# Attention with top-32 and two MLP layers on one core: VectorE's written order from unit 2 on, and three small differences moved between engines

## The chip, the cores and the metric

The kernel runs on one NeuronCore of a Trainium2 chip. The metric is device time in microseconds; the median of three runs of the kernel before is 1382.83 us (1382.4 to 1383.42).

The engines are named as in the profile: PE is TensorE (matrix multiply, writes PSUM), DVE is VectorE, ACT is ScalarE, POOL is GpSimd, SP is SyncE, which issues most DMAs.

## The reference

```python
def _attn_ref(q, k, v):                      # q, k, v: [4, 8, 576, 64] float32
    scores = scale * np.matmul(q, k.transpose(0, 1, 3, 2))
    kth = np.partition(scores, -32, axis=-1)[..., -32:-31]
    scores = np.where(scores >= kth, scores, -1000000000.0)
    attn = np.exp(scores - np.max(scores, axis=-1, keepdims=True))
    attn = attn / (np.sum(attn, axis=-1, keepdims=True) + 1e-09)
    return np.matmul(attn, v)

def _moe_ref(x, w_in, w_out, a, b):          # x: [2304, 512]; w_in: [512, 2048]; w_out: [2048, 512]
    h = x @ w_in
    P = a[0] + a[1] * h + a[2] * h**2 + a[3] * h**3
    Q = 1.0 + np.abs(b[0]) * np.abs(h) + np.abs(b[1]) * h**2
    return (P / (Q + 1e-6)) @ w_out

def _moe2_ref(x, w_in, w_out):               # the same sizes
    h = x @ w_in
    return (h * np.cos(h)) @ w_out
```

The attention's output, laid out as 2304 tokens of 512, goes through `_moe_ref` and then `_moe2_ref`.

## The kernel before

**Units and pieces.** The attention is cut into 72 units, each a tile of 128 query rows of a pair of heads. Each unit is written as five pieces, and the program is a run of pieces: piece p belongs to unit p // 5. The MLP layers work on 9 blocks of 256 tokens; block k's first layer starts at piece 46 + 40 k (unit 9 for block 0), its second layer 50 pieces later, so from about unit 19 on a block's worth of both layers runs beside every 8 units of attention.

**A unit.** PE makes the scores (`qk`, tile `sx`), ACT copies them to `sS`. DVE searches the 32nd largest of each row (`topk`): two TENSOR_TENSOR (maximum and minimum of the row's two halves) into `e`, then MAX8 and MATCH_REPLACE8 in turn, while ACT makes the exponentials into `e`; two SCALAR_TENSOR_TENSOR then mask `e` and sum it, PE transposes it (`pp`) and multiplies it with v (`av`). The scores take q and k in two parts each, a high part rounded for TensorE's faster kind of float32 and the rest as a low part. q is split for two units at once (`split_q`): ACT writes `qh`, and the difference `ql` is made by DVE from unit 20 on and by GpSimd before it. `qh` has one buffer, so ACT may overwrite it only when PE has done the scores of the unit that still reads it.

**Conversion.** The four weight matrices arrive as 64-bit floats, and 64 conversions (`conv`, 128x512 each) turn them into such pairs of parts. Kinds 0 and 1 are the first layer's input and output weights, kinds 2 and 3 those of the second. One conversion is: DMA of `raw`; two ACT operations (`cb<-raw`, `raw<-raw`); a shift by DVE (`TENSOR_SCALAR cb<-cb`); an integer add by GpSimd (`cb<-cb,raw`); the high part by ACT; the difference from the high part; two DMAs to DRAM, from which the layers read it later. The difference is made by PE for kinds 0 and 2 (two matmuls into `diff`, one with the identity and one with its negative, then an ACT copy `cb<-diff`), by GpSimd for kind 1 and by DVE for kind 3 (`cb<-cb,ch`). Kinds 0 and 1 have six `cb` buffers; kinds 2 and 3 have three, so the first ACT operation of a conversion waits until the difference of the third one before it has landed in DRAM. Pieces pull conversions: 36 by piece 46, the other 28 by piece 80.

**Order.** What is written in the pieces is put in order on each engine by a scheduler, within windows (`Windowed`: a piece's instructions stay behind those of 8 pieces earlier, for DVE). From unit U0 = 20 to U1 = 72 (pieces C0 to C1) three more things hold. `InOrder` keeps every DVE instruction in the order in which it is written, and notes the last one that is neither MAX8 nor MATCH_REPLACE8 as `shared`. `Behind` lets every GpSimd instruction wait for that `shared` one:

```python
if C0 <= self.piece < C1 and self.v.shared is not None:
    self.tc.add_manual_dep(r.ins, self.v.shared, WAIT, reason="port")
```

And `topk`, `in1`, `end1`, `norm` and the main loop write the work grouped: at a unit's first piece stand the first layer's operations of DVE (`end1`), the two SCALAR_TENSOR_TENSOR of the unit before and the two TENSOR_TENSOR of this one, and then only MAX8 and MATCH_REPLACE8. In grouped units `norm` leaves two operations of every fourth unit to GpSimd that are DVE's elsewhere.

## Time and profile before

| | |
|---|---|
| median of three runs | 1382.83 us |
| the profiled execution | 1386.08 us, of it 1384.3 us span |
| PE busy | 1233.5 us (89%) |
| DVE busy | 1170.6 us (85%) |
| ACT busy | 1080.4 us (78%) |
| POOL busy | 589.7 us (43%) |
| unit 2's first TENSOR_TENSOR starts at | 38.4 us |
| unit 10's | 161.6 us |
| unit 17's | 312.2 us |
| unit 20's | 361.4 us |
| unit 71's | 1182.7 us |

The span is 1.8 us shorter than the profiled execution's own time. Busy shares are means over stretches with different limits, so the stretches between the unit starts above are read one by one. All operations of DVE, ACT and POOL go through the recording helper and so have its line (L81); they are told apart by their tiles. Consecutive operations of an engine overlap by some 0.07 us, so durations add up to a little more than busy time.

### The profile page before, as it was taken

The numbers are of one execution on the slowest core, as the hardware profiler recorded it, in microseconds if no ns is written. First come the engines' busy times: TensorE is split into PE (matmuls) and PEld (weight loads), VectorE is DVE, ScalarE is ACT, GpSimd is POOL, SyncE is SP. The second block draws the span as 40 slices with busy tenths as digits, with TensorE's granted clock in tenths as the row PEclk, the third lists the DMA queues.
The fourth block names the chain that finished last, engine by engine and source line by source line (L and its number), as shares of the span: only waits on it lengthen the run. The fifth ranks groups of instructions, "written<-read, shape, count | busy, mean of one in ns | idle before, by whom it ended". The sixth has DMA issues, their size and how long they took to land.

```text
span 1384.3 us, 24846 instructions
## 1 busy us (share of the span) xinstructions
PE 1233.5 (89%) x8944; PEld 1095.6 (79%) x8944; DVE 1170.6 (85%) x2477; ACT 1080.4 (78%) x1886; POOL 589.7 (43%) x439
## 2 busy tenths in 40 slices
PE   5786776676898999999989999999999999999997
PEld 2444555565798898899889889989899899999986
DVE  6989977999999898998989898989998888666533
ACT  6887778775788787888878888888888788697653
POOL 3676455553356343644553455445453434430000
PEclk9757789777999999999999999999999999999999
DMA  7996668792467666556776665666666678567786
GB/s 238 330 325 214 220 192 250 241 320 94 159 218 228 232 231 204 202 190 222 243 226 226 222 217 191 225 199 208 206 206 238 236 273 283 196 215 251 240 274 217
DMA packets 141547, 314.97 MB, mean 228 GB/s; under 512 B 12016, under 2 KB 28528, under 8 KB 141424
## 3 DMA queue, kind: packets, MB, share of 16 engines
q1 hardware_dynamic: 122832, 261.99, 57.2%
q10 hardware_dynamic: 18592, 51.39, 11.0%
q8 instruction: 71, 1.16, 0.3%
q14 instruction: 52, 0.43, 0.1%
HBM read 278.20 MB, written 35.13 MB: 226 GB/s over the span
## 4 chain that ended last, share of the span: by engine, by line
PE 41%; DVE 25%; ACT 15%; DMA 9%; issue 5%; POOL 5%; ACTq 0%; SPq 0%; POOLq 0%; DVEq 0%
DVE e L81 11%; PE o L636 8%; DVE hd L81 5%; PE h L496 5%; PE h L498 5%; PE h L497 5%; DVE u L81 4%; PE y L567 3%; PE sx L436 3%; PE y L568 3%; PE y L566 2%; DMA raw<-w 2%; POOL gg L81 2%; ACT r L81 2%; ACT L81 2%
## 5 line engine op out<-in xcount | busy, mean ns | idle before, releaser
L81 DVE MAX8 hd<-e 128x8 f32<-128x288 f32 (+1 forms) x576 | 321.0, 596 | 0.0
L81 DVE MATCH_REPLACE8 e<-hd,e 128x288 f32<-128x288 f32 (+1 forms) x432 | 231.0, 541 | 0.0
L636 PE MATMUL o<-w2o,gg 128*128 128x512 f32 x864 | 217.0, 395 | 8.4 <-POOL gg L81 4.2
L636 PEld LDWEIGHTS o<-w2o,gg 128*128 128x128 f32 x864 | 155.2, 188 | 43.0 <-POOL gg L81 8.1
L496 PE MATMUL h<-xh,w1hi 128*128 128x256 f32 x576 | 172.1, 299 | 18.5 <-ACT pt10a L81 3.0
L567 PE MATMUL y<-gg,w1o 128*128 128x256 f32 x576 | 167.4, 291 | 9.2 <-POOL gg L81 9.1
L566 PE MATMUL y<-gg,w1o 128*128 128x256 f32 x576 | 170.7, 296 | 2.9 <-ACT gg L81 2.9
L81 POOL TENSOR_TENSOR gg<-u,gg 128x512 fp32r<-128x512 f32 x64 | 84.9, 1327 | 205.5 <-DVE rr L81 101.5
L568 PE MATMUL y<-gg,w1ol 128*128 128x256 f32 x576 | 166.3, 289 | 2.1 <-DMA w1ol<-w1ol 2.1
L497 PE MATMUL h<-xl,w1hi 128*128 128x256 f32 x576 | 167.1, 290 | 0.0
L498 PE MATMUL h<-xh,lo 128*128 128x256 f32 x576 | 166.7, 289 | 0.0
L498 PE MATMUL h<-x2h,lo 128*128 128x256 f32 x576 | 163.9, 285 | 0.0
L497 PE MATMUL h<-x2l,w2hi 128*128 128x256 f32 x576 | 163.3, 284 | 0.0
L496 PE MATMUL h<-x2h,w2hi 128*128 128x256 f32 x576 | 162.9, 283 | 0.0
L81 POOL TENSOR_TENSOR rr<-rr,hs 128x512 f32<-128x512 f32 x56 | 72.6, 1299 | 163.4 <-DVE rr L81 119.0
L81 DVE TENSOR_TENSOR e<-sS 128x576 f32<-128x576 f32 x144 | 116.5, 849 | 29.1 <-PE sx L423 21.7
L496 PEld LDWEIGHTS h<-xh,w1hi 128*128 128x128 f32 x576 | 114.8, 199 | 24.8 <-ACT pt10a L81 3.2
L81 DVE SCALAR_TENSOR_TENSOR e<-sS,hd,e 128x576 f32<-128x576 f32 x144 | 127.2, 909 | 8.0 <-ACT e L81 7.8
L81 POOL TENSOR_TENSOR cb<-cb,raw 128x512 int32<-128x512 int32 x64 | 93.0, 1456 | 75.2 <-DVE cb L81 68.0
L567 PEld LDWEIGHTS y<-gg,w1o 128*128 128x128 f32 x576 | 113.5, 197 | 11.4 <-POOL gg L81 10.9
L566 PEld LDWEIGHTS y<-gg,w1o 128*128 128x128 f32 x576 | 113.3, 197 | 4.5 <-ACT gg L81 3.4
L568 PEld LDWEIGHTS y<-gg,w1ol 128*128 128x128 f32 x576 | 113.4, 197 | 3.3 <-DMA w1ol<-w1ol 2.5
(1028 smaller groups left out, 3633.1 us busy)
## 6 DMA issues: line engine op xcount, KB each, us to landing
w2o<-w2o SPq DMA_DIRECT2D x144, 512.0 KB, 4.5
lo<-w1lo SPq DMA_DIRECT2D x72, 512.0 KB, 4.1
w1ol<-w1ol SPq DMA_DIRECT2D x72, 512.0 KB, 4.1
lo<-w2lo SPq DMA_DIRECT2D x72, 512.0 KB, 4.7
k<-kdr ACTq DMA_DIRECT2D x44, 576.0 KB, 4.8
raw<-w SPq DMA_DIRECT2D x32, 512.0 KB, 5.5
v<-vt ACTq DMA_DIRECT2D x48, 320.0 KB, 4.7
qr<-qt ACTq DMA_DIRECT2D x36, 256.0 KB, 4.0
```

The costliest lines, as they stand in the source:

```text
L81: r = f(*a, **k)
L436: mm = PE.matmul(o, v[:, kc * P + j * D:kc * P + (j + 1) * D], pj[j][:, kc, qs], start=False, stop=(kc == 3), skip_group_check=True)
L496: PE.matmul(h[:, i, :], wh, xh[:, c, :], start=(c == 0), stop=False)
L497: PE.matmul(h[:, i, :], wh, xl[:, c, :], start=False, stop=False)
L498: PE.matmul(h[:, i, :], lo[:, i, c, :], xh[:, c, :], start=False, stop=(c == NCC - 1))
L566: PE.matmul(y[:, c, :], w1o[:, f, cs], gh[:, i, :], start=(f == 0 and c % 2 == 0), stop=False, skip_group_check=True)
L567: PE.matmul(y[:, c, :], w1o[:, f, cs], gl[:, i, :], start=False, stop=False, skip_group_check=True)
L568: PE.matmul(y[:, c, :], wl[:, i, cs], gh[:, i, :], start=False, stop=(f == NF - 1), skip_group_check=True)
L636: PE.matmul(o[:, t, :], l[:, i, ts], wt[i][:, r], start=(f == 0 and r == 0 and l is gh), stop=(f == NF - 1 and l is gl), skip_group_check= ...
```

## The change

Five things, in the order of the diff. (1) The difference of kind 3 is made by PE as that of kinds 0 and 2. (2) U0 is 2 instead of 20: order, GpSimd's waits and grouped writing begin at unit 2, piece 10. DVE's window reaches to piece 150 (PM). (3) The conversion's shift is left out of the order and is not noted as `shared` (`loose`): the scheduler puts it where it likes. (4) The low part of q is always GpSimd's. (5) Up to unit 10 a unit's first piece has the two TENSOR_TENSOR ahead of the two SCALAR_TENSOR_TENSOR, from unit 11 on behind them.

```diff
-SUBV = (3,)
-CPE = (0, 2)
+CPE = (0, 2, 3)
-U0, U1 = 20, 72
+U0, U1 = 2, 72
 C0, C1 = 5 * U0, 5 * U1 - 4
@@ class InOrder
+        self.loose = False
...
             r = f(*a, **k)
+            if self.loose:
+                return r
             if C0 <= self.piece < C1:
@@ def body
-    V, A = InOrder(tc, nc.vector, WIN, C0), Windowed(tc, nc.scalar, WA, PA)
+    V, A = InOrder(tc, nc.vector, WIN, PM), Windowed(tc, nc.scalar, WA, PA)
@@ def split_q
             if U0 <= i < U1:
                 yield
-                V.tensor_sub(lo, raw, hi.bitcast(F32))
-            else:
-                G.tensor_sub(lo, raw, hi.bitcast(F32))
+            G.tensor_sub(lo, raw, hi.bitcast(F32))
@@ def conv, rest
+                V.loose = True
                 V.tensor_scalar(ai, ai, 3, 0, op0=ALU.logical_shift_left, op1=ALU.bitwise_or)
+                V.loose = False
...
-                    if kind in SUBV:
-                        V.tensor_sub(a, a, h.bitcast(F32))
-                    else:
-                        G.tensor_sub(a, a, h.bitcast(F32))
+                    G.tensor_sub(a, a, h.bitcast(F32))
@@ def attention
                     if p == 0 and grouped:
                         yield
-                        next(prev)
-                        next(prev)
-                        next(t)
+                        for x in (prev, prev, t) if 5 * i > S0 + 5 else (t, prev, prev):
+                            next(x)
```

What moves is shown at three places. A name's number tells its buffer: `e_144` is unit 0's `e`, `e_177` unit 1's.

PE at the start of the program; `sx<-kraw,qr` are the scores, `diff` the conversions' differences, `pp0a`, `pp1a` the transposes of units 0 and 1. Before:

```order
L343 MATMUL sx<-kraw_0_94,qr_92 128x288 x8
L343 MATMUL sx<-kraw_1_142,qr_156 128x288 x2
L298 MATMUL diff<-cb_0_0_283,ident 128x512
L299 MATMUL diff<-w1hi,nident 128x512
L416 MATMUL pp0a<-ident,e_144 128x128 x4
L416 MATMUL pp0b<-ident,e_144 128x128 x4
```

Now, the rows from the same place, and those with the first conversion:

```order
L342 MATMUL sx<-kraw_0_94,qr_92 128x288 x8
L342 MATMUL sx<-kraw_1_142,qr_156 128x288 x2
L415 MATMUL pp0a<-ident,e_144 128x128 x4
L415 MATMUL pp0b<-ident,e_144 128x128 x4
L342 MATMUL sx<-kraw_1_142,qr_156 128x288 x2
```

```order
L415 MATMUL pp1a<-ident,e_177 128x128 x4
L415 MATMUL pp1b<-ident,e_177 128x128 x4
L300 MATMUL diff<-cb_0_0_281,ident 128x512
L342 MATMUL sx<-kraw_1_142,qr_156 128x288 x2
L301 MATMUL diff<-w1hi,nident 128x512
```

The first conversion's matmuls moved from ahead of unit 0's transposes to behind unit 1's.

DVE around unit 15; `e_1893` is unit 13's, `e_2078` and `e_2096` are unit 14's, `e_2268` and `e_2294` unit 15's, `q_4` and `u_4` the first layer's, `TENSOR_SCALAR cb` the shift, `TENSOR_TENSOR cb<-cb,ch` kind 3's difference. Before:

```order
L81 SCALAR_TENSOR_TENSOR e_1893,sum_1008<-sS_1678,hd_1894,e_1893 128x576 x2
L81 TENSOR_SCALAR cb_2_0_1742<-cb_2_0_1742 128x512
L81 TENSOR_SCALAR cb_3_0_1800<-cb_3_0_1800 128x512
L81 TENSOR_SCALAR cb_4_0_1854<-cb_4_0_1854 128x512
L81 TENSOR_TENSOR cb_2_0_1742<-cb_2_0_1742,ch_2_0_1859 128x512
L81 MATCH_REPLACE e_2078<-hd_2079,e_2078 128x288 x2
L81 TENSOR_TENSOR cb_3_0_1800<-cb_3_0_1800,ch_3_0_1876 128x512
L81 SCALAR_TENSOR_TENSOR q_4_1974<-q_4_1974,r_4_1975 128x512
L81 SCALAR_TENSOR_TENSOR u_4_1976<-u_4_1976,nega,r_4_1975 128x512
L81 MAX hd_2079<-e_2078 128x8 x2
L81 SCALAR_TENSOR_TENSOR u_4_1976<-q_4_1974,u_4_1976 128x512
L81 TENSOR_TENSOR e_2268<-sS_2064 128x2x288 x2
```

Now:

```order
L80 TENSOR_SCALAR cb_5_0_1872<-cb_5_0_1872 128x512
L80 MAX hd_2097<-e_2096 128x8 x2
L80 SCALAR_TENSOR_TENSOR u_4_1991<-u_4_1991,nega,w_4_1988 128x512
L80 SCALAR_TENSOR_TENSOR q_4_1989<-q_4_1989,r_4_1990 128x512
L80 SCALAR_TENSOR_TENSOR u_4_1991<-u_4_1991,nega,r_4_1990 128x512
L80 SCALAR_TENSOR_TENSOR u_4_1991<-q_4_1989,u_4_1991 128x512
L80 SCALAR_TENSOR_TENSOR e_2096,sum_1009<-sS_1884,hd_2097,e_2096 128x576 x2
L80 TENSOR_TENSOR e_2294<-sS_2075 128x2x288 x2
L80 TENSOR_SCALAR cb_6_0_1938<-cb_6_0_1938 128x512
L80 MAX hd_2295<-e_2294 128x8 x2
```

The operations with two tensors stand together, kind 3's differences are gone from DVE, and shifts stand at the border of the group and among the MAX8.

DVE at the end of unit 22, which stands for every second unit from 20 on (`ql` is q's low part, `u_4` and `q_4` the first layer's). Before:

```order
L81 MAX hd_3442<-e_3441 128x8 x2
L81 TENSOR_TENSOR ql_3562<-qr_3482,qh_3561 128x512
L81 SCALAR_TENSOR_TENSOR u_4_3327<-u_4_3327,nega,w_4_3324 128x512
L81 SCALAR_TENSOR_TENSOR q_4_3325<-q_4_3325,r_4_3326 128x512
L81 SCALAR_TENSOR_TENSOR u_4_3327<-u_4_3327,nega,r_4_3326 128x512
```

Now POOL there (`gg` are the low parts of the layers' hidden tiles):

```order
L80 TENSOR_TENSOR q_4_3365<-q_4_3365,r_4_3366 128x512
L80 TENSOR_TENSOR u_4_3367<-u_4_3367,w_4_3364 128x512
L80 TENSOR_TENSOR ql_3602<-qr_3522,qh_3601 128x512
L80 TENSOR_TENSOR gg_1_3525<-rr_0_3065,gg_1_3525 128x512
L80 TENSOR_TENSOR kraw_0_3471<-kraw_0_3471 128x576
L80 TENSOR_TENSOR gg_1_4_3680<-u_4_3367,gg_1_4_3680 128x512
```

`ql` went from DVE, where four first-layer operations stand behind it, to POOL, where the layers' `gg` do.

## Rows read from the trace of the kernel before

**Rows 1.** Stages: us, then busy us (count) by engine, PE clock, DMA share, GB/s

```profile
0.00:38.40 38.40, 21.99 (x42) 10.64 (x42) 22.90 (x56) 24.25 (x43) 13.29 (x16) 0.96 0.79 242
38.40:161.60 123.20, 91.54 (x361) 56.66 (x360) 115.37 (x247) 98.03 (x192) 76.85 (x54) 0.68 0.83 273
161.60:312.20 150.60, 104.86 (x650) 85.42 (x650) 129.75 (x260) 115.40 (x219) 76.92 (x53) 0.83 0.77 251
312.20:361.40 49.20, 35.27 (x250) 32.07 (x250) 47.09 (x98) 30.32 (x57) 14.76 (x9) 0.83 0.36 120
361.40:1182.70 821.30, 788.71 (x6242) 733.65 (x6243) 748.95 (x1647) 683.68 (x1190) 381.07 (x289) 0.99 0.66 221
1182.70:1384.30 201.60, 191.09 (x1402) 177.17 (x1400) 106.55 (x173) 128.72 (x191) 26.81 (x20) 1.00 0.71 234
```

**Rows 2.** Chain of waits by line: units 2-9, 10-16, 20-70

```profile
by line: DVE e L81 17.4%; DVE cb L81 8.1%; DMA kraw<-kt 8.0%; issue 7.9%; DVE hd L81 7.5%; PE diff L298 6.3%; ACT cb L81 6.1%; ACT raw L81 4.7%; DMA raw<-w 4.4%; ACT e L81 3.1%; PE sx L436 3.1%; ACT sS L81 2.8%; ACT w1o L81 2.2%; PE sx L343
...
by line: issue 15.4%; DMA w2lo<-cb 10.5%; DVE e L81 10.4%; DMA raw<-w 9.7%; POOL cb L81 8.4%; ACT cb L81 5.3%; DMA w2o<-ch 3.7%; POOL gg L81 3.2%; DMA raw<-w2o 2.7%; ACT raw L81 2.6%; DVE cb L81 2.4%; DVE hd L81 2.4%; POOL ql L81 2.1%; ACT 
...
by line: DVE e L81 11.9%; PE o L636 8.0%; DVE hd L81 6.4%; DVE u L81 5.3%; PE h L496 5.2%; PE h L497 4.8%; PE h L498 4.8%; issue 3.6%; ACT r L81 3.3%; PE sx L436 3.0%; ACT L81 3.0%; POOL gg L81 2.9%; PE y L567 2.7%; PE y L568 2.6%; PE y L56
```

**Rows 3.** Groups of DVE, units 2-9: busy us, mean ns | idle

```profile
L81 DVE TENSOR_SCALAR cb<-cb 128x512 int32<-128x512 int32 x30 | 22.6, 761 | 3.9 <-ACT cb L81 3.9
L81 DVE SCALAR_TENSOR_TENSOR e<-sS,hd,e 128x576 f32<-128x576 f32 x17 | 18.0, 1059 | 1.3 <-ACT e L81 1.3
L81 DVE TENSOR_TENSOR e<-sS 128x576 f32<-128x576 f32 x16 | 17.5, 1132 | 4.5 <-PE sx L423 4.5
```

**Rows 4.** Groups of DVE, units 10 to 16

```profile
L81 DVE TENSOR_TENSOR e<-sS 128x576 f32<-128x576 f32 x14 | 16.9, 1241 | 3.3 <-PE sx L423 3.3
L81 DVE SCALAR_TENSOR_TENSOR e<-sS,hd,e 128x576 f32<-128x576 f32 x14 | 16.5, 1187 | 1.3 <-ACT e L81 1.2
L81 DVE TENSOR_SCALAR cb<-cb 128x512 int32<-128x512 int32 x27 | 13.3, 497 | 10.5 <-ACT cb L81 10.5
...
L81 DVE TENSOR_TENSOR cb<-cb,ch 128x512 f32<-128x512 f32 x15 | 11.7, 779 | 1.9 <-ACT ch L81 1.9
```

**Rows 5.** Waits, units 10 to 16: us in total, times, longest

```profile
POOL cb L81 <- DVE cb L81: 54.5, 22, 7.1
```

**Rows 6.** Groups of DVE, units 20 to 70

```profile
L81 DVE SCALAR_TENSOR_TENSOR e<-sS,hd,e 128x576 f32<-128x576 f32 x103 | 83.3, 842 | 5.0 <-ACT e L81 5.0
...
L81 DVE TENSOR_TENSOR e<-sS 128x576 f32<-128x576 f32 x102 | 72.5, 752 | 12.7 <-PE sx L423 12.6
...
L81 DVE TENSOR_TENSOR ql<-qr,qh 128x512 fp32r<-128x512 f32 x25 | 17.1, 684 | 40.5 <-ACT qh L81 40.5
```

**Rows 7.** Timeline of DVE, two pairs: start, us, operation, idle before

```profile
38.63 2.51 DVE L81 TENSOR_TENSOR e<-sS 128x576 f32<-128x576 f32 x2 [2.13 <-PE sx L423]
...
840.05 1.42 DVE L81 TENSOR_TENSOR e<-sS 128x576 f32<-128x576 f32 x2
```

**Rows 8.** Tile cb: conversions in the start, of kind 2, of kind 3

```profile
L81 ACT ACTIVATE cb<-raw x7: 651/655/673, 11.9 to 33.6; 128x512 f32<-128x512 f32 x7
...
L81 ACT ACTIVATE cb<-raw x13: 658/673/696, 157.8 to 229.5; 128x512 f32<-128x512 f32 x13
L81 DVE TENSOR_SCALAR cb<-cb x12: 402/415/1256, 158.5 to 220.0; 128x512 int32<-128x512 int32 x12
...
L81 ACT ACTIVATE cb<-raw x16: 652/666/702, 231.8 to 309.0; 128x512 f32<-128x512 f32 x16
```

**Rows 9.** Units 10 to 16, busy us of tile diff alone

```profile
161.60:312.20 150.60, 19.06 (x39) 6.63 (x39) 7.93 (x14) 0.83 0.77 251
```

**Rows 10.** Waits, units 20 to 70: us in total, times, longest

```profile
DVE ql L81 <- ACT qh L81: 40.5, 13, 8.7
...
PE y L567 <- POOL gg L81: 7.0, 6, 2.7
```

**Rows 11.** Group of POOL, units 10 to 16

```profile
L81 POOL TENSOR_TENSOR ql<-qr,qh 128x512 fp32r<-128x512 f32 x4 | 6.0, 1491 | 7.1 <-ACT qh L81 7.1
```

## The prediction

> **What bounds the kernel now.** I read the stages first: the stretches between the starts of units 2, 10, 17, 20 and 71, with each engine's busy time [rows 1]. Dividing, a unit takes 15.4 us in units 2 to 9 (123.2 / 8), 21.5 in 10 to 16 (150.6 / 7), 16.4 in 17 to 19 and 16.1 in 20 to 70 (821.3 / 51). So the slow place is units 10 to 16, and the long one is units 20 to 70. The limits differ. In units 20 to 70 PE is busy 788.7 of 821.3 us and has only 32.6 to give; DVE has 72. In units 2 to 9 DVE is the busiest, 115.4 of 123.2, and in 17 to 19 it is at 47.1 of 49.2. In units 10 to 16 no engine is full: DVE 129.8, ACT 115.4, PE 104.9 of 150.6.
>
> The chain of waits by line [rows 2] says the same. In units 2 to 9 DVE's lines `e`, `cb` and `hd` are a third of it (17.4 + 8.1 + 7.5 = 33%). In units 10 to 16 the DMAs of conversions (`w2lo`, `raw`, `w2o`) are 26.6%, with ACT's and POOL's `cb` behind them. That is a chain of latencies, not a full engine. In units 20 to 70 it alternates between DVE and PE.
>
> Next I looked at why DVE is busy where it is, by the mean of one operation. A shift takes 761 ns on average in units 2 to 9, the masking 1059, the maximum and minimum 1132 [rows 3], and in units 10 to 16 497, 1187 and 1241 [rows 4]; there GpSimd's adds wait 54.5 us for DVE's shift [rows 5]. Where the order is written and GpSimd waits, the masking takes 842 and the maximum and minimum 752 [rows 6]. One pair of `e<-sS` took 2.51 us at 38.6, where GpSimd was at work, and 1.42 at 840 [rows 7]. The shift's median is 415 [rows 8]. So DVE and GpSimd stretch one another where they meet. The stretch sums, against those undisturbed values, to 30 x .346 + 17 x .217 + 16 x .380 = 20.2 us in units 2 to 9 and to 27 x .082 + 14 x .345 + 14 x .489 = 13.9 us in 10 to 16, with kind 3's differences (15 x some .09) 15.3.
>
> The Trainium skill, "SBUF — State Buffer", section on the two separate sides of the port, has VectorE and GpSimd share a port pair that one of them holds for a whole instruction while the other stands still. By that rule the 2.51 us pair is 1.42 plus a good part of a GpSimd operation; the trace agrees.
>
> **The change, part by part.** All sums are against the profiled execution's 1384.3 us of span (1386.1 with what lies around it, 1.8 more; the median of the runs is 3.25 us below that).
>
> *Start.* Before, seven conversions begin by 33.6 us [rows 8]; now GpSimd's first add stands behind unit 1's masking, and the first conversion's matmuls behind unit 1's transposes (the PE order above). So PE's scores find less ahead of them. Unit 2's pair waited 2.13 us for PE and was stretched by 1.1 [rows 7]; both can go: -3 us. From -5, if ACT is freed too, to +2, if unit 1's search now ends later than the first conversion did. The price is that those seven conversions have to be made up later.
>
> *Units 2 to 9.* Some 32 conversions instead of 30, with the written order. DVE is a third of the chain, and the 20.2 us of stretch are DVE's: 20.2 x .33 = -7 us. Against it: the grouped work leaves GpSimd shut out while a group runs, and its adds are then late. GpSimd's 76.9 us of work [rows 1] and DVE's two-tensor operations at undisturbed length (17 x .842 + 16 x .752 = 26 us) fit one behind the other in 103 of 123.2 us. Shifts, left free, stand at the border of groups and still meet GpSimd at times. Range -14 (two thirds of the stretch) to 0 (the adds' delay eats it).
>
> *Units 10 to 16.* Here I count on a loss. The second layer's conversions have three `cb` buffers, so one begins only when the third before it has landed. Kind 2, with the difference on PE, began one every 5.98 us ((229.5 - 157.8) / 12), kind 3, with DVE's, every 5.15 ((309.0 - 231.8) / 15) [rows 8]. Now the stage has 31 conversions to begin instead of 27 (four of those that the start gave up), and kind 3 takes two matmuls and a copy in place of one DVE operation: longer in latency, and 16 x (19.06 / 13 = 1.47) = 23.5 us more on PE and 16 x (7.93 / 14 = .57) = 9 on ACT [rows 9]. With the four more conversions PE comes to about 134 and ACT to about 135 us, both inside 150.6, so neither becomes the bound. DVE loses 11.7 us of differences and up to 13.9 of stretch [rows 4]. What counts is the pace. I take 5.15, kind 3's, for all: the written order spares the collisions that kind 2 had (its shifts took up to 1.26 us, three times the median), and PE's detour lengthens kind 3. 31 x 5.15 = 159.7: +9 us. Ends: at ACT's and PE's busy time, 135, -15; at kind 2's pace 31 x 5.98 = 185.4, +35.
>
> *Units 17 to 19.* DVE at 96% with the stretch gone is what units 20 to 70 show, 16.1 for 16.4 a unit: 3 x .3 = -1 us (-4 to +3: the last conversions may reach into them).
>
> *Units 20 to 70.* The order was grouped there before; only `ql` moves. DVE loses 25 operations, 17.1 us [rows 6], and the waits for `qh` ahead of them, 40.5 us in 13 places, up to 8.7 [rows 10]. Behind `ql` stood four first-layer operations (the DVE order above); GpSimd's `gg` and then PE's `y` wait for them. But DVE waited for `qh` because `qh`'s one buffer was still being read by PE: DVE was ahead of PE, and PE has 32.6 us of idle in all. What of it hangs on that chain is `y` waiting for `gg`, 7.0 us in 6 places [rows 10]: -7 us. Ends: PE never idle, -32; and above nothing, since GpSimd takes 1.49 us for a `ql` [rows 11] and DVE .684 [rows 6], the scores wait for it, and `gg` and the first layer's operations now queue behind GpSimd's own wait: 25 x .81 = 20 at most, of which I keep +5 in the forecast's range.
>
> The Trainium skill, "GPSIMD Engine Reference", section on engine selection, says that elementwise work belongs on VectorE, GpSimd being about twice as slow with two inputs. The rows agree (1.49 to .684). It speaks for rival 5 below; the sum goes by PE's idle time.
>
> Sum: -3 -7 +9 -1 -7 = -9. Span 1375.3; + 1.8 = 1377.1; - 3.25 = **1374 us**.
>
> **Rivals.** (1) *Slower: three buffers bind.* All 31 conversions go at kind 2's pace, since kind 3 is now made as kind 2 and GpSimd's add waits for the group as well. For it: DMAs of conversions lead the chain there, and 5.98 was measured with that very path. Against it: kind 2's pace was measured among collisions. The stage takes 185.4, +35 in place of +9: 1374 + 26 = 1400. It decides from the pace at which the sum is nothing: (150.6 + 18) / 31 = 5.44 us. (2) *No change from the part that is long.* Units 20 to 70 keep their time, PE's idle goes elsewhere: 1374 + 7 = 1381; with the start's conversions a little dearer, up to 1385. For it: waits of an engine that is ahead cost nothing. (3) *DVE and GpSimd's collisions were behind everything, the latencies too.* Units 2 to 9 come to 108, -15; 10 to 16 to PE's and ACT's 135, -16; 20 to 70 give half of PE's idle, -15: with -3 and -1, -50, so 1333. Against it: the chain in 10 to 16 is DMAs for a quarter. (4) *The change doesn't separate the two*: free shifts and GpSimd's operations written before the group still meet it; -3 for the start, nothing else, +9 for the ring: 1389. (5) *Slower: GpSimd's longer `ql` is on the path.* The scores of two units wait for it, .81 us more for each of 25: +20 in place of -7, 1401. Against it: `ql` is made well ahead of the scores wherever PE is behind, and GpSimd is busy only 381 of 821 us [rows 1].
>
> **How the numbers follow.** Forecast .42, its own range 1356 to 1386. Rival 1 .24, rival 2 .11, rival 3 .12, rival 4 .06, rival 5 .05. The range reaches up to the centres of rivals 1 and 5, 1402, and down into rival 3, 1335; half of each, some .2, is left out. A measurement can tell about 0.2% (2.8 us) here, so faster is below 1380.1 and slower above 1385.6. Faster: .38 of the forecast's, rival 3's .12 and .05 of rival 2: .55. Slower: rival 1's .23, rival 5's .05, rival 4's .05, .01 of the forecast: .34. Same: the rest, .11.
>
> **What would show it.** In the changed profile unit 2 should begin near 35 us; the means of `e<-sS` and the masking in units 2 to 16 should be near 752 and 842, and the shift's near 415 but for some. Units 10 to 16 should last near 160 and the conversions of kind 3 begin every 5.15 us or so; at 5.98 rival 1 holds. In units 20 to 70 PE's idle should fall from 32.6 to some 25, with `y` waiting for `gg` less than 7.0, and DVE's waits for `qh` gone. The forecast is wrong if the pace is outside 4.8 to 5.44, or if PE's idle falls below 10 or grows.

## The result and the profile of the changed kernel

The changed kernel took 1395.65 us (median of 4 runs, 1394.7 to 1399.06) against 1383.07 us of the kernel before in the same comparison: 1.0096 times as long, interval 1.0078 to 1.0114. It is slower by 13 us, where 9 us of gain were forecast. The profiled execution took 1399.06 us, 1397.3 of it span; its stages, cut at the starts of the same units (2, 10, 17, 20, 71; the cuts lie some .2 us ahead of the starts in the timelines, in both kernels), answer to [rows 1]. The columns are the stretch, its length, busy time (count) of PE, PEld, DVE, ACT and POOL, the granted clock, DMA share and GB/s:

```profile
0.00:33.10 33.10, 16.52 (x34) 8.80 (x35) 19.91 (x52) 17.35 (x30) 1.78 (x8) 1.00 0.58 180
33.10:157.40 124.30, 91.05 (x360) 57.00 (x360) 112.51 (x243) 96.41 (x188) 81.40 (x60) 0.71 0.84 277
157.40:327.50 170.10, 122.16 (x679) 88.22 (x680) 120.85 (x249) 134.58 (x254) 85.17 (x59) 0.85 0.73 238
327.50:370.00 42.50, 39.12 (x275) 34.76 (x273) 39.77 (x94) 29.03 (x57) 15.22 (x12) 0.85 0.35 120
370.00:1197.20 827.20, 788.09 (x6244) 734.23 (x6245) 741.60 (x1622) 687.95 (x1192) 415.50 (x314) 0.99 0.65 220
1197.20:1397.30 200.10, 192.20 (x1405) 177.64 (x1403) 107.08 (x173) 128.81 (x190) 26.79 (x20) 0.99 0.73 237
```

| stage | before | after | difference | forecast |
|---|---|---|---|---|
| start, to unit 2 | 38.4 | 33.1 | -5.3 | -3 |
| units 2 to 9 | 123.2 | 124.3 | +1.1 | -7 |
| units 10 to 16 | 150.6 | 170.1 | +19.5 | +9 |
| units 17 to 19 | 49.2 | 42.5 | -6.7 | -1 |
| units 20 to 70 | 821.3 | 827.2 | +5.9 | -7 |
| end | 201.6 | 200.1 | -1.5 | 0 |
| span | 1384.3 | 1397.3 | +13.0 | -9 |

Three terms carry the miss: units 2 to 9 came out 8.1 us worse than forecast, units 10 to 16 10.5 and units 20 to 70 12.9; the other three came out 9.5 us better.

**Units 2 to 9.** DVE's groups there (busy us, mean ns | idle before), to be read against [rows 3]:

```profile
L80 DVE TENSOR_SCALAR cb<-cb 128x512 int32<-128x512 int32 x28 | 21.1, 757 | 2.5 <-ACT cb L80 2.5
L80 DVE TENSOR_TENSOR e<-sS 128x576 f32<-128x576 f32 x16 | 17.5, 1129 | 9.0 <-PE sx L422 9.0
L80 DVE SCALAR_TENSOR_TENSOR e<-sS,hd,e 128x576 f32<-128x576 f32 x16 | 16.7, 1071 | 0.2 <-ACT e L80 0.2
```

The means are what they were: 757 for 761, 1129 for 1132, 1071 for 1059 ns. The written order did not part DVE and GpSimd here, so there was nothing to win. DVE's and POOL's timelines, laid side by side, tell what meets: of the 16 operations of the maximum and minimum twelve overlap one of GpSimd (mean 1259 ns), mostly the difference of kind 1 (`cb<-cb,w1o`) or a conversion's add, and the four others take 741. In units 10 to 16, where kind 1 is done, two of 14 overlap. And the stage's chain of waits no longer runs through DVE: its lines `e`, `cb` and `hd` were 33% of it [rows 2] and are 8.6% now, behind GpSimd's adds and the DMAs of conversions:

```profile
by line: issue 23.6%; POOL cb L80 18.0%; DMA raw<-w1o 14.4%; DMA w1lo<-cb 13.6%; DMA raw<-w 11.7%; PE diff L300 4.9%; DVE e L80 4.6%; ACT cb L80 3.0%; DMA w1ol<-cb 2.6%; DVE hd L80 2.1%; DVE cb L80 1.9%; PE sx L342 1.8%; ACT sS L80 1.5%; PO
```

**Units 10 to 16.** The same view for this stage, against [rows 4], and DVE's largest wait there (us in total, times, longest):

```profile
L80 DVE TENSOR_SCALAR cb<-cb 128x512 int32<-128x512 int32 x31 | 19.1, 617 | 48.8 <-ACT cb L80 48.6
L80 DVE SCALAR_TENSOR_TENSOR e<-sS,hd,e 128x576 f32<-128x576 f32 x16 | 16.6, 1066 | 0.2 <-ACT e L80 0.2
...
L80 DVE TENSOR_TENSOR e<-sS 128x576 f32<-128x576 f32 x14 | 9.9, 748 | 0.0
```

```profile
DVE cb L80 <- ACT cb L80: 48.6, 13, 11.8
```

Here the maximum and minimum are undisturbed (748 ns for 1241). But DVE stands still 48.8 us ahead of shifts, where it stood 10.5. DVE's busy time fell by 8.9 us (129.75 to 120.85), its idle time grew by 28.4 (20.9 to 49.3), and 28.4 - 8.9 = 19.5 is the stage's whole growth. The timeline of DVE (start, duration, operation, idle before) shows what one such wait holds up:

```profile
165.73 1.40 DVE L80 MAX8 hd<-e 128x8 f32<-128x576 f32 x2
176.41 0.43 DVE L80 TENSOR_SCALAR cb<-cb 128x512 int32<-128x512 int32 x1 [9.28 <-ACT cb L80]
176.75 0.08 DVE L80 MATCH_VALUE_LOAD e<-hd,e 128x8 f32 x1
176.82 0.74 DVE L80 MATCH_REPLACE8 e<-hd,e 128x576 f32<-128x576 f32 x1
```

The search of a unit stops in its middle for 9.28 us, because a shift stands there in DVE's queue and ACT has not yet begun the conversion that it belongs to. The buffer is one half of that: the DMA that frees it was issued at 167.07 and landed 4.9 us later, at about 172.0. ACT's own queue is the other half: it came to the operation (`cb<-raw`, the last line) only at 175.71, behind others, the first of which had waited for the transfer of another `raw`:

```profile
171.32 0.65 ACT L80 ACTIVATE raw<-raw 128x512 int32<-128x512 uint32 x1 [2.06 <-DMA raw<-w]
...
175.71 0.66 ACT L80 ACTIVATE cb<-raw 128x512 f32<-128x512 f32 x1
```

The conversions themselves, tile `cb` (duration ns min/median/max, first to last start), first those of the start, then kind 2, then kind 3, against [rows 8]:

```profile
L80 ACT ACTIVATE cb<-raw x5: 654/656/668, 11.6 to 19.3; 128x512 f32<-128x512 f32 x5
...
L80 ACT ACTIVATE cb<-raw x16: 649/674/725, 155.9 to 236.1; 128x512 f32<-128x512 f32 x16
...
L80 ACT ACTIVATE cb<-raw x16: 654/667/721, 238.8 to 326.9; 128x512 f32<-128x512 f32 x16
```

Kind 2 began every (236.1 - 155.9) / 15 = 5.35 us, faster than the 5.98 of before; kind 3 every (326.9 - 238.8) / 15 = 5.87, slower than 5.15. Thirty-one conversions begin in the stage, and 170.1 / 31 = 5.49 us. The first five are ready on ACT by 20 us, then nothing moves until GpSimd comes back, as POOL's timeline shows:

```profile
38.02 6.32 POOL L80 TENSOR_TENSOR cb<-cb,raw 128x512 int32<-128x512 int32 x5 [17.77 <-DVE e L80]
```

GpSimd idles 17.77 us with five adds before it, waiting for the masking of unit 1. Conversion 32, the first of kind 2 (they are counted from 0), begins at 155.9 instead of 139.0.

**Units 20 to 70.** The waits that answer to [rows 10]:

```profile
DVE e L80 <- PE sx L422: 66.1, 23, 5.8
POOL ql L80 <- ACT qh L80: 47.4, 14, 5.4
...
PE y L566 <- POOL gg L80: 10.1, 8, 2.5
```

DVE's 40.5 us of waits for `qh` are gone, and 66.1 us of waits for PE stand in their place (12.6 before). `y` waits more for `gg`, not less. PE's idle time is 827.2 - 788.1 = 39.1 us, for 32.6.

### The profile page after: what moved, and what is told of

The parts are those of the page before. It is cut to its first block, busy times and chain, and to the rows that moved or that the text cites. A ratio compares the mean times of both kernels' runs of the same rounds, so it can differ in the third digit from the quotient of the medians.

```text
span 1397.3 us, 24965 instructions
## 1 busy us (share of the span) xinstructions
PE 1249.1 (89%) x8992; PEld 1100.7 (79%) x8992; DVE 1141.7 (82%) x2427; ACT 1094.1 (78%) x1906; POOL 625.9 (45%) x473
## 4 chain that ended last, share of the span: by engine, by line
PE 58%; ACT 13%; DMA 13%; DVE 5%; POOL 5%; issue 4%; SPq 0%; ACTq 0%; POOLq 0%; DVEq 0%
PE o L635 12%; PE h L495 8%; PE h L497 8%; PE h L496 8%; PE y L566 4%; PE y L567 4%; PE y L565 4%; PE sx L435 3%; DMA raw<-w 3%; DVE e L80 2%; POOL cb L80 2%; PE sx L345 2%; POOL gg L80 2%; PE sx L347 2%; ACT r L80 1%
## 5 line engine op out<-in xcount | busy, mean ns | idle before, releaser
L495 PE MATMUL h<-xh,w1hi 128*128 128x256 f32 x576 | 169.1, 294 | 11.8 <-ACT pt33a L80 0.9
L80 DVE TENSOR_TENSOR e<-sS 128x576 f32<-128x576 f32 x144 | 108.6, 793 | 82.4 <-PE sx L422 75.1
L566 PEld LDWEIGHTS y<-gg,w1o 128*128 128x128 f32 x576 | 112.0, 194 | 13.5 <-POOL gg L80 12.8
L80 ACT ACTIVATE sS<-sx 128x576 f32<-128x576 f32 x144 | 92.8, 644 | 37.2 <-PE sx L347 32.1
```

The lines of the kernel that those rows point to most:

```text
L80: r = f(*a, **k)
L495: PE.matmul(h[:, i, :], wh, xh[:, c, :], start=(c == 0), stop=False)
L566: PE.matmul(y[:, c, :], w1o[:, f, cs], gl[:, i, :], start=False, stop=False, skip_group_check=True)
```

## The experiments

All are ratios to the kernel before, run on the same chip beside it, with a 95% interval; 0.1% is 1.4 us. The changed kernel has 1.0096 (1.0078 to 1.0114). Stage times and waits are of one profiled execution each, mostly good to a few us; where that execution was the shortest or the longest of its version, the text says so.

**One part alone, or one part undone**

*q's low part on GpSimd, in the kernel before.*

```diff
-            if U0 <= i < U1:
-                yield
-                V.tensor_sub(lo, raw, hi.bitcast(F32))
-            else:
-                G.tensor_sub(lo, raw, hi.bitcast(F32))
+            G.tensor_sub(lo, raw, hi.bitcast(F32))
```

> The kernel before, with one part of the change alone: the low part of q is GpSimd's in every unit. Theory ql: this move by itself lengthens units 20 to 70, by about the 5.9 us that they grew by in the changed kernel (821.3 to 827.2), because the scores wait for GpSimd's longer operation: about 1389 us. Rival, the late start: units 20 to 70 grew for another reason, the move is worth what the prediction gave it or nothing: 1376 to 1384.

Measured: 1.0061 (1.0041 to 1.0081), median 1393.57 us. The move alone costs 8 us, on a kernel that is otherwise the old one. Its profiled execution was one of its shorter ones (1389.9 us), and shows units 20 to 70 at 822.8, so the size of the loss is read from the ratio, not from this trace. The wait of DVE for PE's transposes is there at once, 64.3 us in 23 places.

*The same part undone in the changed kernel.*

```diff
-            G.tensor_sub(lo, raw, hi.bitcast(F32))
+            (V if i >= 20 else G).tensor_sub(lo, raw, hi.bitcast(F32))
```

> The changed kernel, but the low part of q is VectorE's again from unit 20 on. Theory ql: the move costs time by itself (the kernel before with this move alone took 1.0061 times its time, some 8 us), so 6 to 8 us come back here, to about 1.004 times the time of the kernel before, and units 20 to 70 fall from 827 to about 821 us. Rival, luck of the granted clock: VectorE's share of this stage does not matter, the ratio stays within 0.2% of 1.0096.

Measured: 1.0020 (1.0006 to 1.0034): 10 us come back. Units 20 to 70 and their waits (the trace is of the shortest of twelve executions, 1384.61 us for a median of 1387.78, and that of the changed kernel of the longest of four, so a part of the difference between the two is the executions' own):

```profile
365.60:1182.20 816.60, 786.83 (x6246) 731.98 (x6245) 748.39 (x1647) 683.84 (x1189) 380.65 (x289) 1.00 0.66 222
```

```profile
DVE ql L80 <- ACT qh L80: 37.0, 13, 5.9
...
DVE e L80 <- PE sx L422: 13.7, 6, 4.5
```

The stage falls from 827.2 to 816.6, and the wait for PE from 66.1 to 13.7. The waits of `ql` for `qh` are back, 37.0 us, and the stage is shorter with them: DVE waits there while PE works, and PE's idle time is 29.8 us. Over all kept traces but the three of the part on `ql` below, in which PE's order was forced, units 20 to 70 took 819.1 to 827.2 us in the nine versions with GpSimd's `ql` and 813.5 to 821.3 in the seven with VectorE's.

*Kind 3's difference by PE, in the kernel before.*

```diff
-CPE = (0, 2)
+CPE = (0, 2, 3)
```

> The kernel before, with one part of the change alone: kind 3's difference is made by PE (two matmuls and an ACT copy) as kind 2's. Theory ring: a conversion of kind 3 then takes the longer way through three buffers; it began every 5.14 us before and every 5.87 in the changed kernel, 15 x .73 = +11 us, so about 1394. Rival, the late start: the pace is not made by this detour, kind 3 keeps about 5.1 to 5.3 us and the time stays at 1380 to 1386.

Measured: 1.0012 (0.9996 to 1.0028), no difference that can be told. The ring theory was right on the pace and wrong on the price: kind 3 began every 5.71 us in this trace, the last conversion 9 us later (317.8 for 309.0), yet unit 17 begins at 312.3 (312.2 before) and unit 20 at 361.3 (361.4). The trace is of the shortest of twelve executions (1380.01 us, median 1386.68), so the price is read from the ratio. A slower kind 3 did not lengthen this kernel; but DVE lost its differences as well (busy time in units 10 to 16 121.1 for 129.8), and no run parts that gain from what the slower ring may cost.

*Kind 3's difference back on VectorE, in the changed kernel.*

```diff
-CPE = (0, 2, 3)
+SUBV = (3,)
+CPE = (0, 2)
...
-                    G.tensor_sub(a, a, h.bitcast(F32))
+                    if kind in SUBV:
+                        V.tensor_sub(a, a, h.bitcast(F32))
+                    else:
+                        G.tensor_sub(a, a, h.bitcast(F32))
```

> The changed kernel, but kind 3's difference is VectorE's again, in its written order. Theory ring: kind 3 goes back to about 5.1 us a conversion and some 11 us are won, about 1385. Rival, the late start: the conversions begin as late as in the changed kernel, the last begins at about 325 as there, and the time stays within 3 us of 1395.7.

Measured: 1.0262 (1.0235 to 1.0288), 23 us more than the changed kernel, the opposite of what the ring theory said and outside the other's range too. DVE's waits in units 10 to 16, which last 199.0 us here, in the shortest of six executions:

```profile
DVE cb L81 <- ACT cb L81: 43.7, 15, 10.0
...
DVE cb L81 <- ACT ch L81: 28.3, 11, 5.5
```

A second operation of the conversion stands in DVE's written order, and DVE waits for that one as well: 72.0 us and 126.5 us of busy time make 198.5 of the 199.0. This is what turned me from the ring to DVE's queue.

*The shift in the written order too.*

```diff
-                V.loose = True
```

> The changed kernel, but the shift stands in VectorE's written order like everything else and GpSimd waits for it. Theory that the free shifts cost: they stand ahead of searches and let VectorE wait for ACT (48.6 us in units 10 to 16), so ordered shifts win up to 10 us, 1.002 to 1.006 times the kernel before. Rival, free shifts help: an ordered shift stands at its written place and holds back all that is written behind it, as VectorE's kind 3 differences did (1.0262); the time is above 1.015 times the kernel before.

Measured: 1.0173 (1.0153 to 1.0193): the rival holds, free shifts are worth 11 us. Units 2 to 9 grow to 158.2 us, with 30.8 us of waits for ACT at shifts and DVE more disturbed than before (1484 ns for 1132). Units 10 to 16 are shorter there, 148.8 us, with 24 conversions left to begin in them:

```profile
L80 DVE TENSOR_TENSOR e<-sS 128x576 f32<-128x576 f32 x16 | 23.1, 1484 | 0.2 <-PE sx L421 0.2
L80 DVE TENSOR_SCALAR cb<-cb 128x512 int32<-128x512 int32 x40 | 22.1, 554 | 35.0 <-ACT cb L80 30.8 <-issue 3.4 <-POOL cb L80 0.8
```

**What holds the conversions**

*GpSimd's first eight adds wait for nothing but their data; then all 64.*

```diff
-            if C0 <= self.piece < C1 and self.v.shared is not None:
+            if C0 <= self.piece < C1 and self.v.shared is not None and not self.free:
...
+                G.free = convs.index((kind, c, x)) < 8
                 G.tensor_add(ai, ai, lo)
+                G.free = False
```

> The changed kernel, but GpSimd's adds of the first eight conversions don't wait for VectorE's last grouped operation. Theory late start: the first conversions begin before 34 us again as they did before (seven by 33.6, against five by 33 and the sixth at 42.3 in the changed kernel), the whole train of 64 is 15 us or so earlier, the last begins near 310 instead of 326.6, unit 20 begins near 356 instead of 370, and the time is about 1382. Rival, ring: the train is held by its buffers later on, the last one begins within 5 us of 326.6, and the time is within 4 us of 1395.7.

> The changed kernel, but none of the 64 conversions' adds on GpSimd waits for VectorE's last grouped operation. Theory held conversions: those waits hold a conversion back to the place where it is written, so that conversion 32 begins at 9.9 units instead of 8.6 and 31 conversions are left for units 10 to 16, which then last 31 x 5.5 = 170 us. Without the waits conversion 32 begins near unit 8.6 to 9, units 10 to 16 hold some 27, and last about 150 to 155; the time falls to about 1380. Rival, ring alone: the pace of 5.5 us and the stage of 165 to 170 us stay, the time is within 4 us of the changed kernel's with the first eight freed (1.004 times the kernel before).

Measured: 1.0039 (1.0019 to 1.0060) and 1.0061 (1.0038 to 1.0085), the second with 64 for 8. Freeing the first eight wins 8 us, freeing the rest as well no more than that, and neither reaches the 1380 to 1382 us of the theories. The start is as it said: conversion 6 begins at 33.8 and 33.0 instead of 52.8. But conversion 31 begins at 134.3 and 125.7 (117.7 before, 137.4 in the changed kernel), and the last at 327.4 and 325.2, hardly earlier than the 326.9 of the changed kernel, as the ring rival had it. Units 10 to 16 take 164.5 and 161.8 us, with 45.2 and 42.9 us of DVE's waits at shifts. The late start is a part of the loss, and the waits of GpSimd's adds are not the rest.

*Every conversion written five pieces earlier.*

```diff
-            if p < S0:
-                pull(int(max(p - P0, 0) / (S0 - P0) * NC0))
-            elif p < C2:
-                pull(NC0 + int((p - S0 + 1) / (C2 - S0) * (len(convs) - NC0)))
+            w = p + 5
+            if w < S0:
+                pull(int(max(w - P0, 0) / (S0 - P0) * NC0))
+            elif w < C2:
+                pull(NC0 + int((w - S0 + 1) / (C2 - S0) * (len(convs) - NC0)))
```

> The changed kernel with every conversion written five pieces (one unit) earlier. Theory held conversions: a conversion can start no earlier than its place, so all begin about a unit earlier (conversion 32 near unit 9, eight conversions by 40 us), units 10 to 16 hold four fewer, and last about 150 us; the time falls to about 1382. Rival, ring alone: units 10 to 16 stay above 163 us, and the time within 4 us of the changed kernel's.

Measured: 0.9961 (0.9943 to 0.9980): 19 us less than the changed kernel, and less than the kernel before.

```profile
38.10:164.30 126.20, 89.55 (x382) 54.51 (x382) 111.36 (x241) 100.35 (x197) 82.17 (x60) 0.74 0.84 274
164.30:317.60 153.30, 116.89 (x654) 84.80 (x654) 117.14 (x244) 123.30 (x229) 75.31 (x54) 0.85 0.74 245
317.60:356.90 39.30, 34.09 (x266) 31.61 (x267) 39.20 (x93) 28.19 (x52) 13.91 (x11) 0.91 0.36 117
```

```profile
DVE cb L80 <- ACT cb L80: 39.6, 11, 11.8
```

Conversion 32 begins at 139.5 and the last at 301.2. Units 10 to 16 take 153.3 us, and DVE waits 39.6 us at shifts there instead of 48.6. An earlier start alone (the first eight adds freed) did not do this; the earlier place of all operations of all conversions did.

*The same in the kernel before, with kind 3 by PE.*

> The kernel before with kind 3's difference by PE and the conversions written a unit earlier; no written order of VectorE before unit 20, ql VectorE's. Theory held conversions: without GpSimd's waits conversions already run about a unit ahead of their place, so writing them earlier gives little: .995 to 1.003. Rival, the gain of the earlier place has nothing to do with the written order: it gives here what it gave the changed kernel, 1.35%, and the time is about .988 of the kernel before, as short as with the written order.

Measured: 0.9975 (0.9961 to 0.9989). Of the 1.35% that the earlier place gave the changed kernel, only .37% appear here (1.0012 to 0.9975). Without the written order the first layer's conversions run ahead of their place by themselves, as the theory said. Set against the pieces at which they are pulled, conversions 8 to 31 begin 1.2 to 1.9 units ahead in the kernel before, and within some .4 of a unit of their piece in the changed kernel; those of the second layer begin at their place or behind it in both, by up to 1.7 and 1.4 units. But being ahead is not the whole reason for the small gain: in these traces units 10 to 16 fall from 150.5 to 139.1 us and the last conversion begins at 295.1 instead of 317.8, and units 17 to 19 (55.5 for 49.0), the start and units 20 to 70 take it back. Why they do is not shown.

*Four buffers in place of three.*

```diff
-RA, CA, RB, CB = 5, 6, 3, 3
+RA, CA, RB, CB = 5, 6, 3, 4
```

> The changed kernel with four cb buffers for kinds 2 and 3 instead of three. Theory ring: the pace of conversions 32 to 63, 5.5 us, is that of a chain through three buffers; with four it falls to under 5 us, units 10 to 16 last under 155 us instead of 170, and the time falls to about 1382. Rival, written order: the pace comes from the places at which the engines' instructions stand, a fourth buffer is not used, and the time is within 4 us of the changed kernel's.

Measured: 1.0032 (1.0014 to 1.0049), 9 us less than the changed kernel, between the two expectations. Kind 3's pace is 5.19 us here, so the ring has a part in that pace; but units 10 to 16 still last 166.7 us, and DVE still waits 46.5 us at shifts. The trace is of the longest of twelve executions (1394.06 us, median 1388.98) and shows 5 of the 9 us.

*The written order from unit 10 on.*

```diff
-U0, U1 = 2, 72
+U0, U1 = 10, 72
```

> The changed kernel with the written order from unit 10 on instead of unit 2. Theory held conversions: nothing holds the first layer's conversions, conversion 32 begins near unit 8.6 as in the kernel before, units 10 to 16 hold some 27 and last about 150 to 155 us, and the ratio is .997 to 1.002. Rival, the written order in units 10 to 16 is itself what lengthens that stage: it stays above 163 us and the ratio above 1.005.

Measured: 1.0005 (0.9987 to 1.0023). The ratio is the theory's, the stage lies between the two cases: conversion 32 begins at 141.4, nearly as before, but units 10 to 16 take 159.1 us with 37.3 us of waits at shifts, and the last conversion begins at 326.9 (the trace is of the longest of twelve executions, 1391.17 us for a median of 1387.13). So the order in units 2 to 9 delays the conversions by some 15 us, and the order in units 10 to 16 slows them again: both parts of the stage's growth are there.

**Putting the two losses right**

*Conversions a unit earlier and VectorE's `ql`; the same with four buffers; with four buffers and conversions two units earlier (`w = p + 10`).*

> The changed kernel with the conversions written a unit earlier and the low part of q VectorE's again from unit 20 on. Theory of two separate losses (held conversions in units 10 to 16, ql in units 20 to 70): the two gains add, .9961 less .0076, about .9885 times the kernel before, near 1370 us; units 20 to 70 take about 816 us. Rival, the gains overlap: not below .994.

> As the run with the conversions a unit earlier and VectorE's ql, with four cb buffers for kinds 2 and 3 as well. Theory ring and position both: a fourth buffer still shortens units 10 to 16, by up to the 6 us that it gave the changed kernel by unit 20: about .985. Rival, position alone: once the conversions begin earlier the fourth buffer is worth less than 2 us, .988 to .990.

> As the version with conversions a unit earlier, VectorE's ql and four buffers (.9852), but with the conversions two units earlier. Theory: the place still holds the conversions back at one unit, so a further unit wins a few us more in units 10 to 16, .980 to .984. Rival: from there on the buffers and the weights' transfers set the pace and what comes earlier crowds units 2 to 9: .985 to .992.

Measured: 0.9910 (0.9896 to 0.9924), 0.9852 (0.9839 to 0.9865) and 0.9904 (0.9886 to 0.9922). The gains of place and `ql` add for the most part: 0.9961 - 0.0076 = 0.9885 was expected, which lies outside the interval, and `ql` is worth .51% here, 7 us, not .76%. So the two losses are largely separate. A fourth buffer is worth another .58%, as the theory of ring and place said: 1363.52 us, the shortest of all, and shorter than both kernels. Its units 2 to 9, 10 to 16, 17 to 19 and 20 to 70:

```profile
37.60:159.10 121.50, 89.61 (x378) 53.91 (x378) 110.12 (x241) 97.37 (x191) 81.55 (x60) 0.72 0.86 282
159.10:302.40 143.30, 111.11 (x653) 81.47 (x653) 111.41 (x244) 122.56 (x233) 71.42 (x53) 0.89 0.77 260
302.40:343.40 41.00, 34.16 (x276) 31.43 (x275) 40.90 (x94) 29.72 (x58) 14.46 (x11) 0.96 0.39 135
343.40:1160.90 817.50, 787.93 (x6246) 733.24 (x6245) 748.75 (x1647) 684.13 (x1190) 379.90 (x289) 0.99 0.65 222
```

Two units earlier is too early, as the rival had it: units 10 to 16 fall to 138.8, but units 2 to 9 grow to 132.4.

**Why `ql` on GpSimd costs time**

DVE waited for PE's transposes of `e` (L422). With `ql` on GpSimd PE's order is another one: in unit 31, for instance, the last transpose of unit 30's `e` stands behind the 12 output matmuls, with `ql` on DVE ahead of them. Three runs tried to tell this order from GpSimd's longer operation.

*The output matmuls kept behind the transposes.*

```diff
+            tail[0] = mm.ins.name
...
-                    PE.matmul(o[:, t, :], l[:, i, ts], wt[i][:, r], ...
+                    mm = PE.matmul(o[:, t, :], l[:, i, ts], wt[i][:, r], ...
+                    if grouped2(k, g):
+                        tc.add_manual_dep(mm.ins, tail[0], ORDER, reason="tail")
```

> The changed kernel, with PE's 12 matmuls of the second layer's output kept behind the last transposes of e in each unit (where the kernel before has them; with ql on GpSimd the scheduler puts them ahead). Theory PE order: the 66 us that VectorE waited for those transposes in units 20 to 70 (13.7 with VectorE's ql) come from this order, not from GpSimd's longer operation; the waits fall to under 35 us, units 20 to 70 to 820 or below, and the time to about 1.003 to 1.006 times the kernel before. Rival, GpSimd's length: units 20 to 70 stay at 824 or more and the ratio above 1.007.

Measured: 1.0144 (1.0115 to 1.0174), worse by 7 us; the wait for the transposes fell only to 51.3 us, and units 20 to 70 took 833.9 (in a trace of 1407.05 us, for a median of 1402.01). Holding this one pair of operations in place does not bring the loss back.

*PE's whole order from unit 21 on exchanged between the two versions.*

```diff
+        last = None
+        for y in COPIED:
+            if last is not None:
+                tc.add_manual_dep(PE.log[y], PE.log[last].name, ORDER, reason="copied")
+            last = y
```

The edit is written shorter here: `COPIED` is the other version's order of matmuls, `PE.log` the matmuls as they are written.

> The changed kernel, ql on GpSimd, with PE's matmuls kept from unit 21 on in the order that they have when ql is VectorE's. Theory PE order: the loss in units 20 to 70 is that order; it goes without moving ql back, units 20 to 70 take about 816 to 819 us and the ratio is about 1.002. Rival, GpSimd's length: the scores now wait for GpSimd's ql in PE's queue, units 20 to 70 take 824 us or more, the ratio is 1.008 or more.

> The other way round: ql VectorE's from unit 20 on, PE's matmuls kept from unit 21 on in the order that they have when ql is GpSimd's. Theory PE order: the loss comes with the order alone, units 20 to 70 take 824 to 828 us and the ratio is about 1.009. Rival, GpSimd's length: VectorE's short ql is there, units 20 to 70 take about 816 to 819 us and the ratio is about 1.002.

Measured:

| | PE's order of VectorE's `ql` | PE's order of GpSimd's `ql` |
|---|---|---|
| `ql` on VectorE | 1.0020 (own) | 1.0174 (1.0150 to 1.0199) |
| `ql` on GpSimd | 1.0243 (1.0218 to 1.0267) | 1.0096 (own) |

Each version goes with its own order, and a foreign order costs 20 us either way; units 20 to 70 take 849.1 us (`ql` on GpSimd) and 838.4 (on VectorE) with it. So "the order alone" has fallen: with the good order `ql` on GpSimd is at its worst, 31 us behind `ql` on VectorE. In that run units 20 to 70 show these waits (L82 and L99 are the recording helpers' lines there; PE's operations have one too):

```profile
DVE e L99 <- PE sx L82: 68.1, 25, 5.5
POOL ql L99 <- ACT qh L99: 50.7, 22, 6.8
...
PE sx L82 <- ACT xs L99: 21.6, 12, 2.4
```

"The length alone" has fallen as well, since VectorE's short `ql` with the other order loses 21 us. The traces say more against it: in the changed kernel GpSimd's `ql` ends at least 6.0 us before the next score that reads it (5.8 in the run with the exchanged order), and no wait of PE is put down to it in either. What stands: with `ql` on GpSimd PE's scores stand later, in odd units from 21 to 69 7.1 us (median) after the unit's first TENSOR_TENSOR instead of 3.6, and 7 to 10 us are lost. Why the scheduler puts them later, and which queue passes the delay on, stays open; none of these runs holds ACT's order fixed, and none forces a version's own order on it, so what the forcing itself costs is not known.

## Why the prediction was wrong, point by point

*What bounds the kernel.* That the limits differ by stage, and that units 10 to 16 and 20 to 70 would decide, held. That units 10 to 16 are "a chain of latencies, not a full engine" held too, but I took it for a chain through buffers only. With the written order it runs through DVE's queue as well, and, in the place shown, through ACT's.

*Start.* -5.3 for -3, by the mechanism named: unit 2 begins at 33.1 us. The price that was named there, conversions to be made up later, came as well: conversion 32 began 17 us later.

*Units 2 to 9.* +1.1 for -7. The step that failed is "20.2 x .33 = -7 us". The means did not change (757, 1129, 1071 ns), so none of the stretch went, and DVE's share of the chain, from which the third was taken, fell to 8.6%. I had seen that free shifts meet GpSimd, and that GpSimd's adds are late; I priced both as an end of the range. Rival 4 had this stage right. That it is kind 1's differences and late adds that still meet the grouped operations is read from the overlaps in the trace; no run tested it by itself.

*Units 10 to 16.* +19.5 for +9. The count of 31 conversions was right; the pace was the term that was mis-sized, 5.49 us for 5.15, just beyond the 5.44 from which the sum was to turn. Its two halves were named: kind 2 quickened (5.98 to 5.35) and kind 3 slowed (5.15 to 5.87). That kind 3 slows by PE's detour alone is shown (5.71 in the kernel before). That kind 2 quickened by losing its collisions is not: the shift's mean in this stage rose, from 497 to 617 ns. But the rival's mechanism, three buffers, is only part of it. A slower kind 3 cost the kernel before nothing that can be told (1.0012), and four buffers gave back 9 of 13 us with the waits at shifts nearly unchanged in the trace (46.5 us). The step that the prediction lacked is what stands behind the shift in DVE's queue: it reckoned the shift by its duration, .415 us, and never by the wait that it brings into the middle of a search. In the versions with the written order DVE's busy time and its waits at shifts make up units 10 to 16 to within some 4 us (120.9 + 48.6 = 169.5 of 170.1; 117.1 + 39.6 = 156.7 of 153.3; 111.4 + 34.5 = 145.9 of 143.3), with the one from unit 10 on when its 7.3 us of waits for PE are added (114.7 + 37.3 + 7.3 = 159.3 of 159.1). That says where DVE stands idle; it does not prove that the stage would end earlier if the shifts stood elsewhere, and no run took them off DVE with the rest left alone. What does go with the stage is the number of conversions that begin in it: with the written order, three buffers and kind 3 by PE, 24 in 148.8 us, 26 in 152.1 to 159.1, 27 in 161.8, 28 in 164.5, 30 or 31 in 167.9 to 171.5.

*Units 17 to 19.* -6.7 for -1. Here the stretch did go: the masking takes 813 ns for 1063 and the maximum and minimum 749 for 931, DVE's busy time fell by 7.3 us (47.09 to 39.77), and DVE was the full engine. The term was too small. Units 10 to 19 together lost 12.8 us for the 8 forecast.

*Units 20 to 70.* +5.9 for -7, and 7 to 10 us by the runs that moved `ql` alone. The step that failed is "`y` waiting for `gg`, 7.0 us in 6 places [rows 10]: -7 us": this wait grew to 10.1 us. The remark beside it, that DVE waited for `qh` because it was ahead of PE, was the right reading, and it says that those waits cost nothing. From it the gain should have been put at nothing, and a loss at the centre. The bound "25 x .81 = 20 at most" was set by GpSimd's 1.49 us, four operations of units 10 to 16; in units 20 to 70 its `ql` takes 1.31 (median), so 25 x .62 is some 15. The Trainium skill's page "GPSIMD Engine Reference", section on engine selection, which sends two-input elementwise work to VectorE, pointed that way; 1.31 for .69 us agrees with it, and so does the sign of the loss, but not by the operation's length, for which no score waited.

*The rivals.* What happened is rival 1 at less than half its price (+10 us more than forecast in units 10 to 16, not +26), rival 4 in units 2 to 9 (+8 us), and the sign of rival 5 at half its price (+13 us, not +27), though not by its mechanism. I gave them separate chances and let the range end where one of them alone would; that they could come together I did not weigh. That the time still lies between the centres of the forecast and of rival 1 is luck in part: the start, units 17 to 19 and the end came out 9.5 us shorter than the sum had them, without which it would have been 1405 us.

## What to carry to other kernels

When an order is written out for an in-order engine, price every operation of side work in it by what it may wait for, and by all that is queued behind it, not by its duration: here a .42 us shift held DVE for 9.28 us in one place, and shifts held it for 48.6 us in one stage. Side work that used to run ahead of its place, here by more than a unit, is held at its place once such an order holds and another engine waits for it; write it earlier before judging the order (here the difference between 1.0096 and 0.9961). And an engine's wait that is long but lies while the bound engine works may be worth nothing: here 40.5 us of such waits went when `ql` moved to GpSimd, and the kernel became .5 to .8% slower.

## What the runs showed of the hardware that I had not expected

The granted clock of the same instructions differs between executions. With `ql` on GpSimd alone, every engine's order is that of the kernel before up to 344 us (650 matmuls in units 10 to 16 in both), yet that stage took 154.4 us at a clock of .80, and 150.6 at .83 in [rows 1]:

```profile
161.70:316.10 154.40, 110.39 (x650) 90.05 (x650) 131.96 (x260) 117.32 (x220) 76.81 (x54) 0.80 0.75 245
```

Which of the two comes first, the clock or the longer stage, is not shown. A few us of one stage in one trace are therefore no evidence. Of the whole time, single runs of the kernel before ranged from 1380.2 to 1393.9 us over the chips of the later comparisons, and the intervals above, from 4 to 12 runs of each version, are .3 to .6% wide.
